# Experts' scores cut at each 32-query block, two tiles mirrored, values by pairs of tiles, in a fused attention and mixture-of-experts kernel

## The chip, the cores and the metric

The kernel runs on one core of one Trainium2 chip. The metric is the device time of one execution in microseconds. A core has a matrix engine (TensorE, PE in the profile), a vector engine (VectorE, DVE), a scalar engine (ScalarE, ACT), GpSimd (POOL) and SyncE (SP), which only issues transfers; their instruction streams run in order each and meet by semaphores. Matmuls write into PSUM, which has eight banks of 128 x 512 float32 numbers; VectorE and ScalarE read them from there.

## What is computed

Eight batches. First an attention with eight heads of 64 dimensions: 512 local queries look at neighbours within 32 positions and at 32 global keys, 32 global queries look at everything. Its output, 544 positions x 512 columns for each batch, goes into four "experts": causal attentions over all 544 positions, weighted by a gate that keeps the best two.

```python
# attention
s_ll = np.where(np.abs(pos[:, None] - pos[None, :]) <= 32, scale * q_l @ k_l.T, -1e9)
a_l = softmax(concat([scale * q_l @ k_g.T, s_ll]))
out_l = a_l @ concat([v_g, v_l])
out_g = softmax(scale * q_g @ concat([k_g, k_l]).T) @ concat([v_g, v_l])
# experts, on x = [out_g, out_l] with 512 columns
topk = two largest of x @ w_gate;  w = softmax over these two
for e in range(4):
    q, k, v = x @ wq[e], x @ wk[e], x @ wv[e]        # 64 columns each
    scores = where(causal, scale * q @ k.T, -1e9)
    ye = softmax(scores) @ v @ wo[e]
    out += (weight of e, 0 if not chosen) * ye
```

## The kernel before

The program is recorded as a list of operations, each with the engines that may run it, a cost, a priority and what it reads and writes (class `Plan`, lines 75 to 220). `place` then orders them: again and again it takes the operation that can start first by these costs, for TensorE also weighing the change of array shape and the distance to the oldest operation waiting. Buffers come from rings (`buf`, a tag and a number of copies); a ring with one copy makes the next writer wait until the last reader is done. The eight PSUM banks form one ring. So a change of costs, buffers or operations changes the whole order on every engine.

Work goes in 42 steps. One step handles one pair of heads of the local attention (32 pairs: load, transposes, scores L536, softmax L548 and L551, turning the probabilities L569, values L599, division L603) and, six steps later, a quarter of a batch of the experts. The experts of a batch are two pairs `c`; one matmul pair fills the two halves of the 128 rows with expert 2c and 2c+1. For a batch these are:

- `m_qk`, `m_v` (L733, L762, L773): projections, with weights split into a high and a low part.
- `m_scores` (L854): queries come in four tiles `i` of 128. A tile needs keys 0 to 128(i+1). Each tile's queries are four blocks `u` of 32; each block and each expert is one matmul, 32 queries standing (weights), the keys moving. The blocks lie in four groups of 32 columns of the array, the two experts in its two halves of rows, so eight matmuls sit on eight different parts of the array. Every block of a tile moves all 128(i+1) keys. Tiles 0 and 1 share a pair of banks (`TILES`, line 840).
- `m_softmax`: VectorE adds the mask and takes the minimum of the negated scores (L868), ScalarE takes the exponential (L872), VectorE the reciprocal (L875, L877), GpSimd scales by reciprocal and gate (L886; in the last pair GpSimd or VectorE).
- `m_ptrans`: turns the probabilities by 128-blocks (L569), into a ring `mptw` of three buffers, evicted by ScalarE (L277) or VectorE (L279).
- `m_av` (L921): for each tile and key block, one matmul of 64 value columns (weights) and 128 moving queries for each expert; then the result is split into a high and a low part (L288, L289).
- `m_tail_scores`, `m_tail_av` (L944, L984): the same for the 32 last positions of a batch, in one stacked tile. `m_gates`: the two best experts and their weights, on VectorE.
- `out_tile`, `m_out` (L1003): output projection, copied by ScalarE (L277) and written by one transfer of 128 rows that ScalarE issues (L1010).

Turned local probabilities (`ptw`) have two buffers. The raw weights go through `mptw` at the start.

## Time and profile before

| | |
|---|---|
| median of 3 runs (lowest, highest) | 503.62 us (503.43, 504.33) |
| profiled execution | 505.81 us |
| its span, first to last instruction | 504.0 us |
| TensorE busy, share of the span | 469.3 us, 93% |
| VectorE | 385.7 us, 77% |
| ScalarE | 324.4 us, 64% |
| GpSimd | 281.0 us, 56% |
| mean granted TensorE clock | 0.99 |
| L854, expert scores, TensorE busy | 43.7 us, 1024 instructions |
| L921, expert values, TensorE busy | 41.0 us, 640 instructions |

A float32 matmul stands in the profile as two instructions (two passes). Busy time of TensorE counts time in which at least one matmul is in flight; matmuls overlap, so what an operation costs is read from the distance of starts: the start of the next operation less its own start. In a timeline row the columns are start, length until the last end, engine, line, operation, what it writes and reads, the shape, and the number of instructions merged; in brackets the idle time before and what ended it. In a row of stages each engine has its busy time and its number of instructions.

### The profile page before, as it was taken

Reading aid. Unit: us, or ns where it says so; the run is one execution under the profiler, and the core shown is the slowest. Engines: PE = TensorE matmul, PEld = TensorE weight load, DVE = VectorE, ACT = ScalarE, POOL = GpSimd, SP = SyncE. Lnnn points to the kernel's source line nnn. Section 1 sums busy time; section 2 is a strip of 40 time slices with the busy share of each in tenths; the row PEclk is TensorE's granted clock in tenths of the full one; section 3 lists DMA queues with packets and bytes.
Section 4 is the critical chain, followed back from the end, with each engine's and each line's share of the span. In section 5 each row is a group of like instructions: output and inputs, shape, how many; then the busy total and the mean of one; then the engine's idle time right before and its main releaser. Section 6 shows DMA issues by size and latency. Waiting matters only on the chain.

```text
span 504.0 us, 25622 instructions
## 1 busy us (share of the span) xinstructions
PE 469.3 (93%) x10532; PEld 410.7 (81%) x10532; DVE 385.7 (77%) x1708; ACT 324.4 (64%) x1171; POOL 281.0 (56%) x520
## 2 busy tenths in 40 slices
PE   5787979799999999999989999999999999999985
PEld 3676968589889889889878889898988889888774
DVE  5889768989876997779956998769966976475570
ACT  1668636976756866768746867669757764563662
POOL 5879817869456492928656392837649261331220
PEclk9989989999999999999999999999999999999989
DMA  9955666654246324445146234453022100200203
GB/s 191 220 117 97 140 113 122 115 81 85 35 86 158 68 40 76 106 93 100 32 88 149 49 64 66 108 115 79 4 53 86 28 4 3 85 3 1 86 3 104
DMA packets 181620, 40.98 MB, mean 81 GB/s; under 512 B 176896, under 2 KB 176896, under 8 KB 181504
## 3 DMA queue, kind: packets, MB, share of 16 engines
q1 hardware_dynamic: 169488, 28.70, 31.0%
q10 hardware_dynamic: 12016, 10.65, 6.9%
q8 instruction: 82, 1.34, 1.1%
q14 instruction: 34, 0.28, 0.2%
HBM read 30.42 MB, written 8.91 MB: 78 GB/s over the span
## 4 chain that ended last, share of the span: by engine, by line
PE 76%; DVE 9%; DMA 4%; issue 4%; SPq 4%; ACT 3%; ACTq 1%; POOLq 0%; POOL 0%; DVEq 0%
PE bank L733 18%; PE bank L569 10%; PE bank L1003 9%; PE bank L762 8%; PE bank L921 7%; PE bank L599 6%; PE bank L854 5%; PE bank L536 4%; SPq L295 4%; DVE pm L868 3%; PE bank L703 2%; PE bank L663 2%; DMA qn<-in_q_l_dram 2%; DVE st L548 2%; PE bank L773 1%
## 5 line engine op out<-in xcount | busy, mean ns | idle before, releaser
L886 POOL TENSOR_SCALAR pm<-pm,msm,gate 128x512 f32<-128x512 f32 (+3 forms) x124 | 74.3, 612 | 101.1 <-DVE msm L877 56.1
L279 POOL COPY v<-v 32x512 f32<-32x512 f32 (+1 forms) x192 | 114.5, 596 | 19.8 <-DMA v<-in_v_l_dram 10.0
L551 ACT ACTIVATE st<-st,sm 128x128 f32<-128x128 f32 x256 | 99.7, 392 | 12.3 <-DVE sm L548 12.0
L279 POOL COPY v<-vg 32x640 f32<-32x640 f32 (+1 forms) x96 | 65.3, 680 | 37.6 <-PE bank L703 32.8
L872 ACT ACTIVATE pm<-pm,msm 128x512 f32<-128x512 f32 (+3 forms) x128 | 70.8, 554 | 18.9 <-DVE msm L868 17.8
L548 DVE CUSTOM_DVE_ANT_0 st<-bank,band 128x128 f32<-128x128 f32 x256 | 58.0, 284 | 3.2 <-PE bank L536 3.0
L868 DVE CUSTOM_DVE_ANT_0 pm<-bank,cmask 128x512 f32<-128x512 f32 (+3 forms) x128 | 55.2, 480 | 2.4 <-PE bank L854 2.1
L551 ACT ACTIVATION_READ_ACCUMULATOR st<-st,sm 128x1 f32 x256 | 48.6, 190 | 0.0
L854 PE MATMUL bank<-kt,qt 64*32 64x384 f32 (+3 forms) x1024 | 43.7, 433 | 1.0 <-issue 1.0
L921 PE MATMUL bank<-mptw,vt 128*64 128x128 f32 x640 | 41.0, 281 | 1.7 <-DVE xn L603 0.9
L599 PEld LDWEIGHTS bank<-v,ptw 128*32 128x32 f32 x2048 | 31.3, 112 | 12.8 <-issue 7.7
L536 PE MATMUL bank<-kd,qp 64*32 64x128 f32 x2048 | 39.4, 280 | 2.1 <-issue 2.1
L599 PE MATMUL bank<-v,ptw 128*32 128x64 f32 x2048 | 36.8, 223 | 4.4 <-DVE msm L868 2.5
L277 ACT COPY mptw<-bank 128x384 f32<-128x384 f32 (+1 forms) x50 | 24.2, 520 | 25.6 <-PE bank L921 18.4
L921 PEld LDWEIGHTS bank<-mptw,vt 128*64 128x64 f32 x640 | 36.6, 140 | 3.7 <-issue 2.3
L536 PEld LDWEIGHTS bank<-kd,qp 64*32 64x32 f32 x2048 | 32.1, 108 | 8.6 <-issue 5.0
L733 PE MATMUL bank<-xh,wk_hi 128*128 128x272 f32 x128 | 37.7, 294 | 0.0
L277 ACT COPY ptw<-bank 128x512 f32<-128x512 f32 x34 | 20.0, 594 | 27.1 <-PE bank L569 26.6
L733 PE MATMUL bank<-xl,wk_hi 128*128 128x272 f32 x128 | 37.0, 289 | 0.0
L733 PE MATMUL bank<-xl,wq_hi 128*128 128x272 f32 x128 | 36.9, 288 | 0.0
L733 PE MATMUL bank<-xh,wk_lo 128*128 128x272 f32 x128 | 36.9, 288 | 0.0
L733 PE MATMUL bank<-xh,wq_hi 128*128 128x272 f32 x128 | 36.8, 288 | 0.0
(159 smaller groups left out, 1321.1 us busy)
## 6 DMA issues: line engine op xcount, KB each, us to landing
out_dram<-ot ACTq DMA_DIRECT2D x32, 256.0 KB, 2.1
v<-in_v_l_dram SPq DMA_DIRECT2D x60, 120.0 KB, 2.9
kn<-in_k_l_dram SPq DMA_DIRECT2D x104, 64.0 KB, 2.8
qn<-in_q_l_dram SPq DMA_DIRECT2D x104, 64.0 KB, 2.8
v<-in_v_l_dram SPq DMA_DIRECT2D x31, 64.0 KB, 3.2
kn<-in_k_l_dram SPq DMA_DIRECT2D x8, 128.0 KB, 4.1
qn<-in_q_l_dram SPq DMA_DIRECT2D x8, 128.0 KB, 3.8
ot<-in_q_g_dram SPq DMA_DIRECT2D x8, 64.0 KB, 2.2
```

Of the source, the lines that this page charges most:

```text
L279: ENG[e].tensor_copy(out, in_)
L536: nc.tensor.matmul(sp[h].t[32 * g:32 * g + 32, 128 * t:128 * t + 128], qp.t[rows, 32 * u:32 * u + 32], kd.t[rows, c:c + 128], start=True, ...
L548: op("DVE", 211, lambda e, h=h, t=t, i=i: nc.vector.tensor_tensor_reduce(out=st.t[:, h, t], in0=sp[h].t[:, 128 * t:128 * t + 128], in1=ban ...
L551: op("ACT", 385, lambda e, h=h, t=t, i=i: nc.scalar.activation(st.t[:, h, t], st.t[:, h, t], AF.Exp, bias=sm.t[:, 0, i:i + 1], scale=-1.0, ...
L569: nc.tensor.transpose(two[y].t[:, k, :], block()[rows], ident[rows, rows])
L599: nc.tensor.matmul(xq.t[32 * g:32 * g + 32, t, h, :], pt.t[:, h, 32 * u:32 * u + 32], v.t[:, h, window(u), :], start=True, stop=True)
L733: nc.tensor.matmul(pp.t, w[:, ch, cols], x(part, ch)[:, n], start=(ch == 0 and w is hi and part == 0), stop=(ch == NCH - 1 and part == 1))
L854: nc.tensor.matmul(sp[x].t[32 * u:32 * u + 32, at:at + n], qt.t[rows, q0:q0 + 32], kt.t[rows, :n], start=True, stop=True)
L868: op("DVE", 78 + 1.04 * n, lambda e, x=x, at=at, n=n, i=i, s=s: nc.vector.tensor_tensor_reduce(out=pm.t[:, x, at:at + n], in0=sp[x].t[:, a ...
L872: op("ACT", 280 + 0.83 * n, lambda e, x=x, at=at, n=n, s=s: nc.scalar.activation(pm.t[:, x, at:at + n], pm.t[:, x, at:at + n], AF.Exp, bia ...
L886: lambda e, x=x, at=at, n=n, i=i, s=s: ENG[e].tensor_scalar(pm.t[:, x, at:at + n], pm.t[:, x, at:at + n], sm.t[:, 3, s:s + 1], gate.t[:, i ...
L921: nc.tensor.matmul(yp.t[64 * x:64 * x + 64, 128 * i - n0:128 * i - n0 + 128], vt.t[:, j, 64 * (2 * c + x):64 * (2 * c + x) + 64], flat[:, ...
```

## The change

1. Scores. A block `u` of tile `i` moves only 128i + 32(u+1) keys. In tiles 0 and 1 (`MIRRORED`) the blocks go to the column groups in reverse: block 3 in group 0, block 0 in group 3. Their rows stay reversed, block by block, through softmax, turning and values up to the output. A second mask (`rmask`) and a mirrored copy of two columns of the gates (four GpSimd copies a batch) go with that.
2. Tiles are grouped anew: tile 3 alone, tiles 2 and 0 in one pair of banks, tile 1 alone. Steps 0 and 2 of a batch take tile 3 and tile 1, steps 1 and 3 take tiles 2 and 0.
3. Values. Turned probabilities lie in two buffers with one copy each, `ptu` for tiles 3 and 2 and `ptl` for tiles 1 and 0, with the two tiles of a pair side by side for each key block. One matmul moves both tiles, 256 queries, where both need the key block, and 128 for the last one.
4. Output. Tiles 0 and 1 are written by four transfers of 32 rows each, issued by SyncE; tiles 2 and 3 as before by ScalarE.
5. At the start a zeroed buffer is multiplied into all eight banks, since parts of a bank are no longer written by every tile before they are read.
6. The raw weights go through the ring `pm`, the gate's weights through `msm`; `ptw` has one buffer; the costs given to the planner change with the work.

```diff
-    TILES = (((0, 0), (1, 128)), ((2, 0),), ((3, 0),))
+    TILES = (((3, 0),), ((2, 0), (0, 384)), ((1, 0),))
+    TURNS = ((3,), (2,), (1, 0))
+    MIRRORED = (0, 1)
...
-                n = 128 * (i + 1)
-                for u in range(4):
+                for g in range(4):
+                    u = 3 - g if i in MIRRORED else g
+                    n = 128 * i + 32 * (u + 1)
                     for x in range(2):
...
-                        nc.tensor.matmul(sp[x].t[32 * u:32 * u + 32, at:at + n], qt.t[rows, q0:q0 + 32],
+                        nc.tensor.matmul(sp[x].t[32 * g:32 * g + 32, at:at + n], qt.t[rows, q0:q0 + 32],
                                          kt.t[rows, :n], start=True, stop=True)
-        op("PE", 20 + 1.68 * sum(128 * (i + 1) for i, _ in TILES[t]), f, r=[kt, qt], w=sp, shape="scores")
+        op("PE", 20 + 1.68 * (464, 416, 208)[t], f, r=[kt, qt], w=sp, shape="scores")
...
-                for i in some:
-                    pt, where = pts[i]
-                    flat = pt.t.rearrange("p a j q -> p (a j) q")
-                    for j in range(i + 1):
+                for big, pt in zip(some, pts):
+                    at = Y_AT[big] - n0
+                    for j in range(big + 1):
+                        width = 256 if j < big else 128
                         for x in range(2):
-                            nc.tensor.matmul(yp.t[64 * x:64 * x + 64, 128 * i - n0:128 * i - n0 + 128],
+                            nc.tensor.matmul(yp.t[64 * x:64 * x + 64, at:at + width],
                                              vt.t[:, j, 64 * (2 * c + x):64 * (2 * c + x) + 64],
-                                             flat[:, where[x, i, j], :], start=(j == 0), stop=(j == i))
+                                             pt.t[:, x, 2 * j:2 * j + width // 128, :].rearrange("p s q -> p (s q)"),
+                                             start=(j == 0), stop=(j == big))
...
+        if i in MIRRORED:
+            dsts = [(out[b, 128 * i + 96 - 32 * g:128 * i + 128 - 32 * g, :], slice(32 * g, 32 * g + 32)) for g in range(4)]
+        else:
+            dsts = [(out[b, 128 * i:128 * i + 128, :], slice(0, 128))]
+        out_tile(y, lambda part, c: M[b, "yo"][part].t[:, c, at:at + 128], dsts, "SP" if i in MIRRORED else "ACT")
...
-            for x in {0: [(old, 1, 2)], 1: [(old, 1, 0), (old, 1, 1)], 2: [(cur, 0, 2)], 3: [(cur, 0, 0), (cur, 0, 1)]}[r]:
+            for x in {0: [(old, 1, 0), (old, 1, 2)], 1: [(old, 1, 1)], 2: [(cur, 0, 0), (cur, 0, 2)], 3: [(cur, 0, 1)]}[r]:
...
-        ptw = PR[k, "pt"] = buf("ptw", [128, 2, SL])
+        ptw = PR[k, "pt"] = buf("ptw", [128, 2, SL], 1)
...
+    def clear_banks():
+
+        zero = buf("pm", [128, 512], 3, F32R)
+        op("DVE", 350, lambda e: nc.vector.memset(zero.t.bitcast(F32), 0.0), w=[zero])
+        some = [ps([128, 512], "zero") for _ in range(8)]
+
+        def f(e):
+            for bank in some:
+                nc.tensor.matmul(bank.t, zero.t[:, :128], zero.t, start=True, stop=True)
+        op("PE", 2600, f, r=[zero], w=some)
```

Lines of the changed program differ: L854 becomes L870, L868 L885, L872 L889, L536 L544, L569 L577, L599 L607, L603 L611, L663 L671, L703 L711, L921 L955, L984 L1018, L1003 L1037, L1010 L1044.

The planner's order changes on all engines. Three places follow. TensorE first, in the middle of the program, where the values of a batch's second pair of experts are formed. Before, they follow a turn of probabilities (`ident,pm` turns an expert tile), with local values (L599), global values (L703) and the tail's values (L984) ahead, each in a bank of its own:

```order
L569 MATMUL bank_65<-ident,pm 128x64
L569 MATMUL bank_68<-ident,pm 128x64
L599 MATMUL bank_66<-v,ptw 32x64 x32
L703 MATMUL bank_71<-v,longt 32x64 x20
L984 MATMUL bank_67<-vt,longt 32x64 x20
L921 MATMUL bank_64<-mptw,vt 64x128 x20
L569 MATMUL bank_70<-ident,xn 128x64
L569 MATMUL bank_69<-ident,xn 128x64
```

The same place now:

```order
L544 MATMUL bank_65<-kd_79,qp 32x128
L544 MATMUL bank_64<-kd_79,qp 32x128
L607 MATMUL bank_71<-v,ptw 32x64 x32
L711 MATMUL bank_68<-v,longt 32x64 x20
L1018 MATMUL bank_71<-vt,longt 32x64 x20
L955 MATMUL bank_68<-ptl,vt 64x256 x2
L955 MATMUL bank_68<-ptl,vt 64x128 x2
L955 MATMUL bank_68<-ptu,vt 64x256 x6
L955 MATMUL bank_68<-ptu,vt 64x128 x2
```

The values now follow score matmuls (L544, the last of a bunch that began with tiles 3 and 1), and L1018 and L955 write into the banks that L607 and L711 used just before.

VectorE next: what follows the local masks (L548) in the bunch of score matmuls that also holds the tail's scores. Before, the masks of tiles 0 and 1 come first, in a bank of their own, then tile 2:

```order
L875 TENSOR_SCALAR msm<-msm 128x2
L519 STREAM_TRANSPOSE qp<-qn 128x512
L877 RECIPROCAL msm<-msm 128x2
L868 ISA pm,msm<-bank_66,cmask 128x128
L868 ISA msm 128x1
L868 ISA pm,msm<-bank_65,cmask 128x128
L868 ISA msm 128x1
L868 ISA pm,msm<-bank_66,cmask 128x256
L868 ISA msm 128x1
L868 ISA pm,msm<-bank_65,cmask 128x256
```

Now tiles 2 and 0 share a pair of banks, and both of a bank's masks must be through before it is free:

```order
L892 TENSOR_SCALAR msm<-msm 128x2
L527 STREAM_TRANSPOSE qp<-qn 128x512
L894 RECIPROCAL msm<-msm 128x2
L885 ISA pm,msm<-bank_64,cmask 128x384
L885 ISA msm 128x1
L885 ISA pm,msm<-bank_68,cmask 128x384
L885 ISA msm 128x1
L885 ISA pm,msm<-bank_64,rmask 128x128
L885 ISA msm 128x1
L885 ISA pm,msm<-bank_68,rmask 128x128
```

Tile 1's masks have moved ahead of the local ones, and bank_64 is released by its 128-wide mask, after both 384-wide ones.

Last, ScalarE at the end of the program (`ot` is an output tile; four transfers of 32 rows are the tail's). Before:

```order
L277 COPY ot<-bank_67 128x512
L277 COPY ot<-bank_69 128x512
L1010 DMA out_dram<-ot 32x512 x4
L1010 DMA out_dram<-ot 128x512
L277 COPY ot<-bank_68 128x512
L277 COPY ot<-bank_70 128x512
L1010 DMA out_dram<-ot 128x512 x2
L277 COPY ot<-bank_65 128x512
L1010 DMA out_dram<-ot 128x512
```

Now:

```order
L277 COPY ot<-bank_69 128x512
L1044 DMA out_dram<-ot 32x512 x4
L277 COPY ot<-bank_71 128x512
L277 COPY ot<-bank_68 128x512
L277 COPY ot<-bank_70 128x512
L1044 DMA out_dram<-ot 128x512
L277 COPY ot<-bank_67 128x512
L1044 DMA out_dram<-ot 128x512
```

Two tiles' transfers have left ScalarE; they stand as eight of 32 rows at the end of SyncE's list.

## What was predicted

> **What bounds the kernel now.** I read the page first, then the busy time by stage, then TensorE's and VectorE's timelines through one batch.
>
> ```profile
> span 504.0 us, 25622 instructions
> PE 469.3 (93%) x10532; PEld 410.7 (81%) x10532; DVE 385.7 (77%) x1708; ACT 324.4 (64%) x1171; POOL 281.0 (56%) x520
> PE 76%; DVE 9%; DMA 4%; issue 4%; SPq 4%; ACT 3%; ACTq 1%; POOLq 0%; POOL 0%; DVEq 0%
> ```
>
> TensorE is busy for 93% of the span and holds 76% of the chain. The shares differ by stage (columns: PE, weight loads, VectorE, ScalarE, GpSimd, then granted clock, DMA share and GB/s):
>
> ```profile
> 180.00:240.00 60.00, 58.78 (x1337) 52.55 (x1336) 49.91 (x220) 40.51 (x148) 37.23 (x68) 1.00 0.39 80
> 420.00:480.00 60.00, 60.00 (x964) 50.60 (x966) 35.20 (x133) 30.32 (x89) 15.55 (x29) 1.00 0.10 37
> 480.00:504.00 24.00, 16.76 (x213) 14.04 (x205) 8.80 (x35) 10.27 (x31) 2.65 (x4) 0.93 0.16 55
> ```
>
> In the middle TensorE is full, but VectorE is at 83%. From about 400 us, when local attention has run out, VectorE has room and TensorE alone sets the pace. The last 24 us are a chain of short steps. Inside a batch VectorE's load is bunched: every score bank must be drained by it. This is TensorE through the densest bunch of score matmuls, and the same bunch one batch later:
>
> ```profile
> 221.96 1.09 PE L854 MATMUL bank<-kt,qt 64*32 64x512 f32 x16
> 222.84 1.12 PE L536 MATMUL bank<-kd,qp 64*32 64x128 f32 x63
> 223.73 1.72 PE L854 MATMUL bank<-kt,qt 64*32 64x128 f32 x46
> 225.01 1.30 PE L944 MATMUL bank<-kt,qt 64*32 64x512 f32 x12
> 227.80 1.10 PE L599 MATMUL bank<-v,ptw 128*32 128x64 f32 x64 [0.50 <-DVE msm L868]
> 228.72 0.75 PE L703 MATMUL bank<-v,longt 128*32 128x64 f32 x40
> 229.40 2.40 PE L921 MATMUL bank<-mptw,vt 128*64 128x128 f32 x40
> 231.73 0.28 PE L569 MATMUL bank<-ident,st 64*128 64x64 f32 x2
> 279.41 1.09 PE L854 MATMUL bank<-kt,qt 64*32 64x512 f32 x16
> ```
>
> A batch takes 57.45 us (279.41 less 221.96). At 227.80 TensorE had waited for a bank that VectorE's masks (L868) had to free. VectorE in that bunch:
>
> ```profile
> 223.25 0.69 DVE L868 CUSTOM_DVE_ANT_0 pm<-bank,cmask 128x512 f32<-128x512 f32 x1
> 223.87 0.69 DVE L868 CUSTOM_DVE_ANT_0 pm<-bank,cmask 128x512 f32<-128x512 f32 x1
> 224.48 0.28 DVE L548 CUSTOM_DVE_ANT_0 st<-bank,band 128x128 f32<-128x128 f32 x1
> 226.24 0.70 DVE L519 STREAM_TRANSPOSE qp<-qn 128x512 f32<-128x512 f32 x1
> 226.91 0.27 DVE L868 CUSTOM_DVE_ANT_0 pm<-bank,cmask 128x128 f32<-128x128 f32 x1
> 228.01 0.56 DVE L868 CUSTOM_DVE_ANT_0 pm<-bank,cmask 128x384 f32<-128x384 f32 x1
> 228.96 0.17 DVE L554 TENSOR_SCALAR sm<-sm 128x8 f32<-128x8 f32 x1
> ```
>
> It runs without a gap. Start to start, a 512-wide mask costs 0.62 us (223.87 less 223.25), a 384-wide one 0.48 (228.01 to 228.96 for two), eight local masks and a small step 1.76 (224.48 to 226.24), the transpose with a small step 0.67. Two 128-wide and two 256-wide masks take 1.10 (226.91 to 228.01); at 0.21 and 0.35 that fits.
>
> **The change part by part.** TensorE's prices come from another stretch, where nothing waits:
>
> ```profile
> 258.40 2.40 PE L921 MATMUL bank<-mptw,vt 128*64 128x128 f32 x40
> 260.74 0.46 PE L569 MATMUL bank<-ident,xn 64*128 64x64 f32 x8
> 261.13 1.53 PE L854 MATMUL bank<-kt,qt 64*32 64x128 f32 x48
> 262.45 1.07 PE L663 MATMUL bank<-kd,kq 64*32 64x128 f32 x25
> 263.32 0.30 PE L536 MATMUL bank<-kd,qp 64*32 64x128 f32 x2
> 263.34 0.20 PE L663 MATMUL bank<-kd,kq 64*32 64x32 f32 x3
> ```
>
> Scores. The 512-wide tile takes 0.88 us (222.84 less 221.96), the three others, 768 columns, 1.32 (262.45 less 261.13): 2.20 us for 1280 columns, 1.72 ns a column. With each 32-query block cut at its own end and the mirrored tile behind the plain one, each of the four column groups moves 672 columns for tiles 3 and 1 and 416 for tiles 2 and 0: 1088, so 1.87 us and 0.33 less. That holds only if a group goes on while its neighbours still work. The last two rows speak for it: all of L663 stands ahead of L536 in the program, yet two matmuls of L536, on parts of the array that L663 leaves free, start at 263.32, before three of L663 at 263.34. So the price lies between 0 and -0.33 for each of 16 pairs of experts; I take the full -5.3 us. The Trainium skill says otherwise (TensorE: Matmul & The Clock Gate, Part 3, The mechanism): matmuls start and end in program order, with no reordering. By that rule the widest block holds the rest and this term is about 0; the two rows contradict it.
>
> Products with the values. 40 matmul passes become 24, but the columns moved stay 20 blocks of 128. They take 2.34 us (260.74 less 258.40); at the scores' 1.72 ns a column (0.86 a pass) 20 x 128 columns would be 2.20. So the gain is between 0 and -0.14 a pair, and a change of array shape lies in the same 0.14. I take -0.03, -0.5 in all.
>
> Changes of shape. The new order has 153 stretches of one array shape on TensorE where the old had 165. At 0 to 0.14 each, 0.1 taken: -1.2 us. TensorE's work falls by 7.0 us, about 0.9 a batch.
>
> Waits in the bunches. The old order had three bunches a batch, the new has two, each with tiles 3, 1, a local pair, tiles 2 and 0, and a second local pair (32 L536 matmuls, 0.89 us from 222.84 to 223.73). In the first, the values of the local pair need the bank of tiles 2 and 0, which is free after VectorE's 1.29 (223.25 less 221.96) + 1.23 (tile 3) + 0.70 (tile 1) + 1.76 + 0.67 + 0.96 (tile 2) + 0.21 = 6.8, with the signal 6.9 us. Before, that point came at 5.84 (227.80 less 221.96), without the second local pair. 6.9 less 0.9 is 6.0: no gain here, so 0.2 beside the 0.33 that I counted as saved, +0.5. In the second, the tail's product is put into the very bank that L611 must empty first (bank_71 in the order). L611 comes after 1.29 + 1.23 + 0.70 + 1.76 + 0.67 + 0.48 = 6.1 and takes about as long as a 512-wide mask: 6.8. TensorE, unhindered, is there after 1.87 + 1.78 (two local pairs) + 0.87 (L663, 262.45 to 263.32) + 0.92 (L599) + 0.68 (L703) = 6.1: a wait of 0.7 to 0.8. Then the output projection follows the expert product at once; its low half stands on VectorE behind the other half of the local masks, two 512-wide copies and the rest of tiles 2 and 0, by the same rates at 12.0, where TensorE is ready at 11.5: +0.5. Against this stand 0.5 of small waits that the old layout had. Sum +1.3 a batch, for the six batches beside which local attention runs: +7.8 us. It is the least certain term: +0.6 if ScalarE's copies let VectorE move up, +2.2 if the halves of a tile come later still.
>
> The end. These rows carry it:
>
> ```profile
> 482.50 0.60 ACT L872 ACTIVATE pm<-pm,msm 128x384 f32<-128x384 f32 x1
> 485.08 0.15 DVE L877 RECIPROCAL msm<-msm 128x2 f32<-128x2 f32 x1
> 484.46 0.52 PE L569 MATMUL bank<-ident,long 64*128 64x64 f32 x10 [1.10 <-ACT long L960]
> 486.15 0.61 PE L569 MATMUL bank<-ident,pm 64*128 64x64 f32 x12 [0.79 <-POOL pm L886]
> 487.79 3.60 PE L921 MATMUL bank<-mptw,vt 128*64 128x128 f32 x40
> 491.33 0.33 PE L630 MATMUL bank<-ident,turned 128*128 128x128 f32 x1
> 488.00:490.00 2.00, 2.00 (x22) 2.00 (x22) 0.54 (x2) 0.37 (x1) 0.00 (x0) 0.50 0.00 0
> 498.25 0.40 PE L1003 MATMUL bank<-wo_hi,yl 128*128 128x512 f32 x1
> 500.55 0.58 ACT L277 COPY ot<-bank 128x512 f32<-128x512 f32 x1 [0.63 <-ACT ot L277]
> 501.16 0.34 ACTq L1010 DMA_DIRECT2D out_dram<-ot  x1
> ```
>
> TensorE waits 1.10 and 0.79 us, and the clock is 0.50 while the last expert product runs, 3.54 us (487.79 to 491.33) for 2.34. That is 3.1 us that an earlier softmax could take away. The last exponential ends at 483.1, but its reciprocal starts at 485.08, behind two long VectorE steps. In the new order tile 3's scores of this pair stand ahead of the previous output projection, and the reciprocal directly behind the masks. I take -2.3, between 0 and -3.1. Behind the last matmul (498.65) ScalarE starts its last copy at 500.55, being busy with copies and five DMA issues; two of the five tiles now leave by SyncE, but as eight issues, 0.34 each by the last row, so I take only -0.4.
>
> The start:
>
> ```profile
> 3.45 0.66 PE L420 MATMUL bank<-ident,ot 64*128 64x64 f32 x4 [3.45 <-DMA ot<-in_k_g_dram]
> 10.18 1.08 PE L506 MATMUL bank<-ident,qn 128*128 128x128 f32 x4 [1.54 <-DMA qn<-in_q_l_dram]
> ```
>
> Clearing the banks is eight 512-wide matmuls, 3.2 us at the 0.40 of the row at 498.25 and 6.4 at half clock. TensorE has no data before 3.45 us and waits for loads again at 10.18, so at most the first transposes move. I take -0.3, between +1 and -1.5, since early matmuls may also raise the clock sooner.
>
> The rest costs nothing. The mirrored gates (four small GpSimd copies a batch, queued ahead of GpSimd's value copies and of the mirrored tiles' scaling) and the second mask's setup fall into the 23 us of 60 that GpSimd has free. Eight more SyncE issues a batch, 2.7 us, each waiting for a copy by ScalarE, stand ahead of loads that run two pairs ahead; without that lead a late load would hold VectorE's transposes by the issue time. The evictions of the turned probabilities keep their runs of 64 elements. Single buffers for them cost nothing where the product stands ahead of the next turn, as it does in the new order; elsewhere the eviction, and the next turn on its bank, would wait for the product.
>
> Sum: -5.3 - 0.5 - 1.2 + 7.8 - 2.7 - 0.3 = -2.2. The profiled execution took 505.81 us (span 504.0) and would take 503.6; the runs' median, 503.62, becomes 501.4.
>
> **The rivals.** (a) The bunches do not wait longer than before: without the +7.8 it is 493.6; half of it gives 497.5. For it: VectorE's total work is unchanged. Against: the gapless VectorE rows above, and eight banks for 14 uses before L607. Chance 0.21 for 497.5 or below. (b) Slower: VectorE's draining of the bunches becomes the bound. If each batch waits 1 us more than I count (2.3), that is +6: 507.4. It decides from 1.67 us a batch on, where the sum passes zero. For it: chain and wait row above run through L868. The Trainium skill warns of this (TensorEngine Tiling, PSUM Bottleneck): tiling speeds TensorE, not the emptying of PSUM; the wait at 227.80 agrees. Chance 0.23. (c) The groups keep to program order, so the cut scores save nothing: half of the 5.3 lies in waits anyway, so 504.0. The rows at 263.32 speak against it. Chance 0.05. This is what the in-order rule of the Trainium skill, weighed above, would give. (d) Gains and waits cancel within 1 us: 0.16. The forecast's own case, 498 to 502.6: 0.35.
>
> **How the numbers follow.** About 1 us (0.2%) is what a measurement here tells from no change. Faster by more: the forecast and (a), 0.56; same 0.16; slower (b) and (c), 0.28. The range, 496.5 to 506.5, leaves out the full form of (a) and the far end of (b), about 0.1 each.
>
> **What would show it.** Right: 1.87 us a pair for the scores, rows of a later tile starting on one column group before the earlier tile has ended on another; L611 releasing TensorE before the tail's product, the values' wait for L885, 57.8 us a batch; no half clock near the end. Wrong: a batch of 56.5 us or less (then the waits are mis-sized), or over 59, or scores still at 2.2.

## The result and the profile after

The kernel before took 503.2 us (median of six runs, 502.02 to 504.33), the changed kernel 508.4 (six runs, 505.35 to 509.63): a ratio of 1.0099, 95% interval 1.007 to 1.0127. The change made the kernel about 5 us slower. The forecast was 501.4, faster, with a range up to 506.5.

The profiled execution of the changed kernel, at 505.35 us, is the fastest of its six; that of before, at 505.81, lies above all six of its own. So the two profiles differ by 0.5 us while the medians differ by 5, and stages are compared below rather than spans. Two executions of one later kernel (the last experiments' blocks of 32) ran at a lower clock and over 1% longer than its others, one of them the profiled one; they are left out of its median, and its profile is not used. The page after: its span, TensorE's busy time, the chain that ended last by engine, and the queue that carries instructions (packets, MB, share of the 16 DMA engines).

```profile
span 502.9 us, 25258 instructions
PE 464.2 (92%) x10284; PEld 404.1 (80%) x10284; DVE 385.1 (77%) x1715; ACT 320.8 (64%) x1164; POOL 291.0 (58%) x558
PE 61%; DVE 13%; POOL 7%; issue 6%; DMA 5%; SPq 4%; ACT 3%; ACTq 1%; DVEq 0%; POOLq 0%
q8 instruction: 80, 1.31, 1.1%
```

TensorE's work fell by 5.1 us, from 469.3. But TensorE's share of the chain fell from 76 to 61%, VectorE's rose from 9 to 13, GpSimd's from 0 to 7 (only 2 in a second profile, below), and "issue", time in which an engine waits for nothing that the profile shows, from 4 to 6.

Three whole batches beside local attention, from the first matmul of the tail's value projection (L773, now L781) to the same matmul three batches later. First before, then after (columns: length, then busy time of TensorE, weight loads, VectorE, ScalarE, GpSimd, granted clock, DMA share, GB/s):

```profile
176.42:348.35 171.93, 167.66 (x3935) 149.46 (x3935) 141.11 (x624) 119.77 (x438) 103.67 (x190) 1.00 0.41 84
```

```profile
172.66:349.74 177.08, 165.59 (x3839) 146.94 (x3839) 138.95 (x628) 118.17 (x435) 106.17 (x201) 1.00 0.40 82
```

A batch took 57.3 us before and takes 59.0 now, though TensorE is busy for 0.7 us less in it. The other batches differ less or the other way: the first two took 61.7 and 57.7 us before and take 59.0 and 58.3 now, in these two profiles. What TensorE waited for in these windows (total us, times, longest), before:

```profile
PE bank L599 <- DVE msm L868: 1.8, 3, 0.7
PE bank L984 <- issue: 1.4, 1, 1.4
PE bank L921 <- issue: 0.5, 1, 0.5
PE bank L599 <- issue: 0.2, 1, 0.2
```

and after:

```profile
PE bank L711 <- issue: 4.4, 3, 1.6
PE bank L638 <- DVE ptw L279: 2.3, 3, 0.8
PE bank L607 <- DVE msm L885: 2.2, 3, 0.8
PE bank L544 <- issue: 1.2, 3, 0.5
PE bank L607 <- issue: 0.9, 1, 0.9
```

Waits for VectorE rose from 1.8 to 4.5 us in three batches, waits for "issue" from 2.1 to 6.5. This is TensorE through the second bunch of one of these batches, each row a run of like matmuls with their number:

```profile
247.75 1.37 PE L870 MATMUL bank<-kt,qt 64*32 64x416 f32 x32
248.90 1.11 PE L544 MATMUL bank<-kd,qp 64*32 64x128 f32 x63
249.78 0.40 PE L870 MATMUL bank<-kt,qt 64*32 64x288 f32 x1
249.79 0.27 PE L544 MATMUL bank<-kd,qp 64*32 64x128 f32 x1
249.79 0.91 PE L870 MATMUL bank<-kt,qt 64*32 64x288 f32 x26
250.48 0.27 PE L671 MATMUL bank<-kd,kq 64*32 64x128 f32 x1
...
252.11 1.07 PE L544 MATMUL bank<-kd,qp 64*32 64x128 f32 x54 [0.27 <-issue]
253.11 1.10 PE L607 MATMUL bank<-v,ptw 128*32 128x64 f32 x64
254.03 0.33 PE L711 MATMUL bank<-v,longt 128*32 128x64 f32 x9
255.76 0.60 PE L711 MATMUL bank<-v,longt 96*32 96x64 f32 x28 [1.40 <-issue]
256.20 0.77 PE L1018 MATMUL bank<-vt,longt 128*32 128x64 f32 x39
256.90 0.87 PE L955 MATMUL bank<-ptl,vt 128*64 128x256 f32 x8
...
261.47 0.44 PE L638 MATMUL bank<-ident,turned 128*128 128x128 f32 x2 [0.78 <-DVE ptw L279]
```

At 255.76 TensorE had stood still for 1.40 us in the middle of L711, with nine of that operation's matmuls done and no operand missing. From the wait that ended at 252.11 to that one there are 54 + 64 + 9 = 127 matmuls, each with a weight load: about 256 instructions. The page's instruction queue carries 80 packets of 16 KB. With all entries of TensorE's queue in the trace numbered in order of start (matmuls, weight loads and the few control instructions), nearly all its "issue" waits of at least 0.3 us end at one place in 256. This is a count over the trace's records, for the two kernels and for the runs of the next section; the fetches are the packets of the instruction queue:

```
kernel                    waits   us   at 193 or 194 mod 256   closest two fetches, us
before                      10    9.5           9                      3.36
changed kernel              13   12.6          13                      3.29
changed, second profile     15   15.3          15                      3.31
half of VectorE's masks     19   20.3          19                      3.32
64 matmuls ahead            16   16.1          15                      3.31
local scores two blocks      5    3.8           5                      3.34
same, kernel before          5    3.1           4                      3.38
scores uncut                13   14.2          13                      3.27
two blocks and uncut         7    6.3           6                      3.32
old handing out             15   15.3          14                      3.29
blocks of 64 (last)          9    8.3           9                      3.37
blocks of 64, before        11    9.9          10                      3.36
clearing alone, before      11   10.7          11                      3.31
```

The fetches fit these waits one by one: all 143 that end at this place end 1.15 to 1.86 us after the transfer of a packet has ended (median 1.39). In the changed kernel's first profile the 13 packets concerned start 0.6 to 2.8 us after the block before theirs was entered, and that block then takes 3.2 to 5.4 us, wait included; no block passes in under 3.1. The few waits elsewhere stand 2 us or more after any transfer: one of 0.8 us in the kernel before, which leaves 8.7 of its 9.5.

So the theory tested below, called the code theory: TensorE's program comes in blocks of 256 instructions. The next block is mostly fetched only once the present one has been entered, and 3 to 4 us pass until it can be run. Where 128 matmul passes and their weight loads take less than that, TensorE waits at the block's end. A local pair's scores are 64 matmuls in 0.88 us, its values another 64 in 0.92, so the bunches are where this binds, and the new order makes two dense bunches a batch of three looser ones. The rival, the VectorE theory, is the forecast's rival (b): VectorE's draining of the score banks sets the length of the bunches. The Trainium skill describes blocks of this size (Runtime: NRT & Kernel Launch, Instruction fetch mechanics), fetched by the sequencer's own queue, and calls their cost mostly hidden; the size agrees with the packets, the hiding doesn't agree with these waits.

### The profile page after: what moved, and what is told of

The parts are those of the page before. It is cut to its first block, busy times and chain, and to the rows that moved or that the text cites. A ratio compares the mean times of both kernels' runs of the same rounds, so it can differ in the third digit from the quotient of the medians.

```text
span 502.9 us, 25258 instructions
## 1 busy us (share of the span) xinstructions
PE 464.2 (92%) x10284; PEld 404.1 (80%) x10284; DVE 385.1 (77%) x1715; ACT 320.8 (64%) x1164; POOL 291.0 (58%) x558
## 4 chain that ended last, share of the span: by engine, by line
PE 61%; DVE 13%; POOL 7%; issue 6%; DMA 5%; SPq 4%; ACT 3%; ACTq 1%; DVEq 0%; POOLq 0%
PE bank L741 17%; PE bank L1037 9%; PE bank L577 8%; PE bank L770 7%; POOL v L279 6%; PE bank L607 5%; PE bank L955 4%; SPq L295 4%; DVE pm L885 4%; PE bank L870 4%; PE bank L544 2%; DVE st L556 2%; DMA qn<-in_q_l_dram 2%; DMA v<-in_v_l_dram 2%; PE bank L711 1%
## 5 line engine op out<-in xcount | busy, mean ns | idle before, releaser
L905 POOL TENSOR_SCALAR pm<-pm,msm,gate 128x512 f32<-128x512 f32 (+3 forms) x125 | 75.6, 620 | 79.7 <-DVE msm L894 61.0
L889 ACT ACTIVATE pm<-pm,msm 128x512 f32<-128x512 f32 (+3 forms) x128 | 70.5, 552 | 20.8 <-DVE msm L885 20.6
L279 POOL COPY v<-vg 32x640 f32<-32x640 f32 (+1 forms) x96 | 67.6, 704 | 22.5 <-PE bank L711 17.6
L544 PE MATMUL bank<-kd,qp 64*32 64x128 f32 x2048 | 42.1, 275 | 4.9 <-issue 4.4
L607 PE MATMUL bank<-v,ptw 128*32 128x64 f32 x2048 | 39.0, 229 | 6.3 <-DVE msm L885 3.0
L506 POOL COPY kd<-kq 128x160 f32<-128x160 f32 x32 | 10.1, 320 | 57.2 <-PE bank L671 35.2
L607 PEld LDWEIGHTS bank<-v,ptw 128*32 128x32 f32 x2048 | 33.0, 115 | 12.3 <-DVE msm L885 4.1
L544 PEld LDWEIGHTS bank<-kd,qp 64*32 64x32 f32 x2048 | 32.7, 106 | 9.8 <-issue 6.9
L885 DVE CUSTOM_DVE_ANT_0 pm<-bank,cmask 128x512 f32<-128x512 f32 (+1 forms) x64 | 37.5, 615 | 2.2 <-PE bank L870 1.6
L870 PE MATMUL bank<-kt,qt 64*32 64x96 f32 (+15 forms) x1024 | 37.8, 393 | 1.1 <-issue 0.7
L770 PE MATMUL bank<-wv_hi,xh 128*128 128x260 f32 x128 | 36.4, 285 | 0.5 <-ACT ptw L277 0.5
L741 PE MATMUL bank<-xh,wq_lo 128*128 128x272 f32 x128 | 36.9, 288 | 0.0
```

Of the source, the lines that this page charges most:

```text
L279: ENG[e].tensor_copy(out, in_)
L544: nc.tensor.matmul(sp[h].t[32 * g:32 * g + 32, 128 * t:128 * t + 128], qp.t[rows, 32 * u:32 * u + 32], kd.t[rows, c:c + 128], start=True, ...
L607: nc.tensor.matmul(xq.t[32 * g:32 * g + 32, t, h, :], pt.t[:, h, 32 * u:32 * u + 32], v.t[:, h, window(u), :], start=True, stop=True)
L741: nc.tensor.matmul(pp.t, w[:, ch, cols], x(part, ch)[:, n], start=(ch == 0 and w is hi and part == 0), stop=(ch == NCH - 1 and part == 1))
L770: nc.tensor.matmul(pv.t, x(part, ch)[:, 128 * i:128 * i + 128], w[:, ch, :], start=(ch == 0 and part == 0 and w is hi), stop=(ch == NCH - ...
L870: nc.tensor.matmul(sp[x].t[32 * g:32 * g + 32, at:at + n], qt.t[rows, q0:q0 + 32], kt.t[rows, :n], start=True, stop=True)
```

## The experiments

**The changed kernel again.** No edit.

> The changed kernel itself once more, for a second profiled execution: the first had a span of 502.9 us, but the timed runs' spans went from 502.9 to 507.2. Code theory (TensorE's program reaches it in blocks of 256 instructions, of which only the next is fetched ahead, and no two fetches of the first trace start less than 3.29 us apart; every wait of TensorE of over 0.5 us for nothing that the profile shows stands at such a block's end): a longer execution differs by these waits, and they stand at the same instructions; 13.7 us of them in the first, 15 to 18 in one that takes 507. VectorE theory (its drain of the score banks holds TensorE): the waits for VectorE differ, 9 us in the first, 12 to 14 in one of 507, those at the blocks' ends don't. Time 506 to 509 for both.

506.63 us (505.14 to 508.28; ratio 1.0076, interval 1.005 to 1.0103). The second profiled execution had a span of 506.4, 3.5 longer than the first. TensorE's longest waits in it:

```profile
PE bank L711 <- issue: 6.3, 5, 1.7
PE bank L544 <- issue: 5.0, 8, 1.1
PE bank L607 <- DVE msm L885: 2.7, 4, 0.8
PE bank L607 <- issue: 2.7, 3, 1.1
PE bank L638 <- DVE ptw L279: 2.6, 4, 0.8
```

In the first execution the same rows were 4.6, 4.4, 3.0, 2.2 and 2.6. The three for "issue" grew by 2.8 in all, the two for VectorE fell by 0.3, and the waits of 0.3 us and more stand again at the blocks' ends. All "issue" waits together grew from 13.8 to 16.3 us, most of the 3.5 us that set these two executions apart.

**Fewer instructions, same columns**, in the changed kernel and in the one before. Half of the local scores are computed with wrong queries.

```diff
-            for t in range(4):
+            for t in (0, 2):
...
-  nc.tensor.matmul(sp[h].t[32 * g:32 * g + 32, 128 * t:128 * t + 128],
-                   qp.t[rows, 32 * u:32 * u + 32], kd.t[rows, c:c + 128],
+  nc.tensor.matmul(sp[h].t[32 * g:32 * g + 32, 128 * t:128 * t + 256],
+                   qp.t[rows, 32 * u:32 * u + 32], kd.t[rows, c:c + 256],
```

> Local attention's score matmuls two blocks at a time: half as many, each 256 columns wide instead of 128, so the columns moved stay and 2048 of TensorE's 20600 instructions go (8 blocks of 81). Half of the local scores are thereby computed with the wrong queries. Order and costs of the plan are as in the changed kernel. Code theory: the waits at the blocks' ends in the bunches shrink by half a block a local pair where they bind, so 8 to 12 us less than the changed kernel, 497 to 501. VectorE theory: VectorE's work is untouched, so within 1 us of the changed kernel.

> The same edit to the kernel before (half of the local scores wrong). Code theory: it has 15.7 us of waits at blocks' ends where the changed kernel has 19.8, in three lighter bunches a batch, so it gains less: 4 to 7 us, 496 to 499, and the distance between the two kernels falls from 5.2 to at most 2 us. VectorE theory: unchanged, 503, and the distance stays 5.

The changed kernel: 493.44 us (492.42 to 493.91; ratio 0.9807, interval 0.9782 to 0.9832). The kernel before: 495.34 (493.21 to 496.64; 0.9844, 0.9816 to 0.9872). The edit took 13.2 us from the changed kernel (beside its 506.63 of the same session) and 7.9 from the other, more than expected of both. (The 15.7 and 19.8 us in the second expectation are more than the 9.5 and 12.6 of the table; counted at the weight loads, the idle time at the block ends is 15.2 and 19.2.) These matmuls themselves cost the same: in the lightened changed kernel a pair's 32 run from 244.62 to 245.49.

```profile
244.62 1.14 PE L544 MATMUL bank<-kd,qp 64*32 64x256 f32 x32
245.49 0.94 PE L870 MATMUL bank<-kt,qt 64*32 64x288 f32 x29
```

That is 0.87 us for 32 where 64 took 0.88 (248.90 to 249.78). What went are the waits; the lightened changed kernel's longest:

```profile
PE bank L607 <- DVE msm L885: 3.2, 4, 0.8
PE bank L1018 <- issue: 2.7, 5, 1.0
...
PE bank L1018 <- DVE xn L611: 1.7, 4, 0.5
```

The wait for VectorE's masks (L607 for L885) is as long as before, and the kernel is 13 us faster. With the code lightened the changed kernel is the faster of the two by 1.9 us; the two intervals overlap, so the sign is likely and not settled. That the forecast's gain, 2.2, lies near it is chance: it set 10.0 us of savings against 7.8 of waits for VectorE.

**Scores uncut.** Every block has its tile's full width again; order and costs stay.

```diff
-                    n = 128 * i + 32 * (u + 1)
+                    n = 128 * (i + 1)
```

> The changed kernel with every block's scores at the full width of its tile again (128, 256, 384 or 512 columns), mirrored tiles, pairs, order and costs kept. The trace's prices put 0.33 us a pair of experts on it, 5.3 us in all. Code theory: the bunches end when their code has come, so in the six batches beside local attention the wider matmuls fill waits, and only the start and the last two batches pay: 1 to 3 us more than the changed kernel. Rival (the cut saved its full price, and something else cost more): 4.5 to 5.5 us more, 513.

508.03 us (505.39 to 510.16; ratio 1.0096, 1.0063 to 1.0129), 1.4 above the changed kernel of the same session, with overlapping intervals. The cut's 5.3 us of passes are worth 1.4 or less in time. The same edit on the lightened kernel:

> The changed kernel with both edits of the first four runs: local scores two blocks at a time (half of them wrong) and the experts' scores at full width. With the code lightened the bunch is no longer held by it everywhere, so the cut should be worth more than the 0.5 us that it was worth in the changed kernel. Code theory: 2 to 5 us above the 493.4 of the kernel with the cut, 495.5 to 498.5. If the cut is hidden by something else (VectorE's drain of the same banks): within 1 us of 493.4.

495.25 us (495.01 to 497.81; ratio 0.9862, 0.9834 to 0.9889), 1.8 above 493.44: just under the expected 2 to 5. The cut is worth little more there, so the code isn't all that swallows it. The waits for VectorE at L607 are 3.2 us with and without the cut; what else hides the remainder was not tried.

**The experts' scores handed out as before.** Only the steps at which the tiles are asked for go back.

```diff
-  {0: [(old, 1, 0), (old, 1, 2)], 1: [(old, 1, 1)], 2: [(cur, 0, 0), (cur, 0, 2)], 3: [(cur, 0, 1)]}
+  {0: [(old, 1, 0)], 1: [(old, 1, 2), (old, 1, 1)], 2: [(cur, 0, 0)], 3: [(cur, 0, 2), (cur, 0, 1)]}
```

> The changed kernel with its experts' scores handed out over the steps as the kernel before had them: tile 3 alone in one step, tiles 2, 0 and 1 in the next (it was tiles 3 and 1, then 2 and 0). Everything else of the change stays; the plan makes a new order of it. Code theory: the blocks of 256 instructions that pass in under 3.6 us become fewer, some 3 to 8 us of the waits at their ends go: 500 to 504. If the cost lies in the cut, the mirrored tiles or the pairs of tiles themselves, it stays: 506 to 509.

503.31 us (501.14 to 506.43; ratio 1.0007, 0.9984 to 1.003): the loss is gone. It came with the new handing out, not with the cut, the mirrored tiles, the pairs or the clearing, which all stay here. The trace bears out the expected mechanism in the middle of the program alone. The same three batches:

```profile
176.02:348.42 172.40, 167.35 (x3837) 144.93 (x3838) 136.66 (x621) 122.12 (x441) 106.63 (x202) 1.00 0.42 84
```

A batch takes 57.5 us, with 2.5 us of "issue" waits in the three where the changed kernel has 6.5, and 1.4 of waits for VectorE for 4.5. Over the whole program the waits at block ends didn't fall: 14.1 us, beside 12.6 and 15.3 in the changed kernel's two profiles, because the start and the first two batches hold more of them. What fell there are the waits for VectorE, to 5.0 us from 12.9 and 11.9. So this run shows where the loss came from, but not that the block ends alone made it.

**VectorE's masks halved.** ScalarE's exponential reads a constant over the full width, so its own work stays; the experts' probabilities are wrong.

```diff
-  out=pm.t[:, x, at:at + n], in0=sp[x].t[:, at:at + n], in1=mask,
+  out=pm.t[:, x, at:at + n // 2], in0=sp[x].t[:, at:at + n // 2], in1=mask[:, :n // 2],
...
-  pm.t[:, x, at:at + n], pm.t[:, x, at:at + n], AF.Exp, ...
+  pm.t[:, x, at:at + n].rearrange("p (j k) -> p j k", k=128),
+  ident.unsqueeze(1).to_broadcast([128, n // 128, 128]), AF.Exp, ...
```

> The changed kernel with VectorE's work on the experts' scores halved: it masks half of each tile's columns, and ScalarE takes the exponential of a constant over the whole width, so its work stays; the probabilities are wrong. About 16 us of VectorE's 385 go, all of them in the bunches. VectorE theory: TensorE's waits for VectorE there (3.0 us for the reciprocals behind the masks, 2.6 us at the transposes of the tail, 0.6 for the scaled heads) go, and the time falls by 5 to 9 us, to 499 to 502. Code theory: the bunch still needs its blocks, so a wait that goes at one place comes back at the next block's end: 0 to 3 us less, 504 to 507.

507.98 us (505.77 to 511.49; ratio 1.0108, 1.0073 to 1.0143): no gain at all. Its page and its waits:

```profile
PE 461.9 (92%) x10284; PEld 402.3 (80%) x10284; DVE 368.5 (73%) x1715; ACT 321.3 (64%) x1164; POOL 292.0 (58%) x558
```

```profile
PE bank L711 <- issue: 7.1, 5, 1.7
PE bank L544 <- issue: 5.2, 8, 1.4
PE bank L607 <- issue: 4.9, 5, 1.6
PE bank L638 <- DVE ptw L279: 2.4, 4, 0.7
```

VectorE lost 16.6 us of work and TensorE its 3.0 us of waits for the masks. The three waits for "issue" grew from 11.2 to 17.2. In the bunch shown above the same matmul, nine into L711, now waits 1.67 us instead of 1.40:

```profile
255.85 0.60 PE L711 MATMUL bank<-v,longt 96*32 96x64 f32 x28 [1.67 <-issue]
```

TensorE reaches the block's end sooner and the block comes no sooner. This removes the drain of the score banks as the cause of the loss. (The wait of L638, for the eviction of turned probabilities, is no mask's and stayed: 2.4 us beside 2.6.)

**Blocks moved by half a block.** 64 small matmuls ahead of the bank clearing.

```diff
+            for _ in range(64):
+                nc.tensor.matmul(some[0].t[:, :32], zero.t[:, :128], zero.t[:, :32], start=True, stop=True)
```

> The changed kernel with 64 more matmuls of 32 columns ahead of the bank clearing, 128 instructions, which is half a block; they can delay the start by up to 3 us, the rest of the order is the same. Code theory: all block ends move by half a block: the waits that stood 194 instructions into the count stand at other matmuls (those of 1.5 to 1.9 us at L711 vanish there and appear at L544 or L607, half a block off), still at 194 modulo 256 of all instructions; the time changes by -3 to +6 us beyond the start. VectorE theory, or any cause in the data: the waits stay at the same matmuls and the time moves by the start's delay alone, 0 to 3 us.

512.71 us (510.02 to 515.03; ratio 1.0198, 1.0167 to 1.0228). The time tells little, since the added matmuls took far longer than expected (below). The places tell much; the bunch shown above, in this kernel:

```profile
263.50 1.04 PE L544 MATMUL bank<-kd,qp 64*32 64x128 f32 x54
264.47 0.35 PE L607 MATMUL bank<-v,ptw 128*32 128x64 f32 x9
265.28 0.93 PE L607 MATMUL bank<-v,ptw 128*32 128x64 f32 x52 [0.46 <-issue]
266.00 0.22 PE L711 MATMUL bank<-v,longt 128*32 128x64 f32 x1
266.03 0.23 PE L607 MATMUL bank<-v,ptw 128*32 128x64 f32 x3
266.06 0.77 PE L711 MATMUL bank<-v,longt 128*32 128x64 f32 x39
267.07 0.69 PE L1018 MATMUL bank<-vt,longt 128*32 128x64 f32 x33 [0.24 <-DVE xn L611]
269.28 0.32 PE L1018 MATMUL bank<-vt,longt 128*32 128x64 f32 x7 [1.52 <-issue]
```

The waits at L544 and L711 are gone from here. They stand in L607 and L1018, 63 and 64 matmuls later, with 52 + 1 + 3 + 39 + 33 = 128 matmuls between them. Counted in instructions they stand where they stood, at 193 or 194 modulo 256. Nothing in the data moved, only the count.

**Towards a better version.** The old handing out while local attention runs, the new one from the step where it has run out; then the same with the experts' scores in blocks of 64 queries, half as many matmuls for 32 more columns.

```diff
+  ({0: [(old, 1, 0), (old, 1, 2)], 1: [(old, 1, 1)], 2: [(cur, 0, 0), (cur, 0, 2)], 3: [(cur, 0, 1)]} if not at(s) else
+   {0: [(old, 1, 0)], 1: [(old, 1, 2), (old, 1, 1)], 2: [(cur, 0, 0)], 3: [(cur, 0, 2), (cur, 0, 1)]})
```

```diff
-                for g in range(4):
-                    u = 3 - g if i in MIRRORED else g
-                    n = 128 * i + 32 * (u + 1)
+                for g in range(2):
+                    u = 1 - g if i in MIRRORED else g
+                    n = 128 * i + 64 * (u + 1)
```

> The kernel with the old handing out of the experts' scores (503.3 us) while local attention runs, and the change's (tiles 3 and 1, then 2 and 0) from the step on where it has run out. The end of the changed kernel had no wait of over 0.4 us and no half clock, that of the other one a wait of 2.23 us and a last expert product of 3.57 us for 2.31. Code theory: the dense bunches are gone in the batches and the last ones hold no local matmuls, so both gains stand: 2.5 to 3.5 us less than 503.3, 499.8 to 500.8. If the changed order brings its waits into the last two batches too: 502.5 to 505.

> The same, with the experts' scores in blocks of 64 queries instead of 32: half as many of these matmuls, 1024 instructions or 4 blocks less, and 32 columns more a column group for each of the two halves of the tiles, 0.11 us a pair of experts by the trace's 1.72 ns, 1.8 us in all. The mirrored tiles are turned and written by 64 rows. Code theory: 8 blocks less were worth 14.1 us in the changed kernel and 7.9 in the kernel before, so 4 blocks in the same bunches are worth 3 to 6 us, less the columns: 1 to 4.5 us less than the kernel in blocks of 32, 496 to 499.5. If instructions cost nothing: 1 to 2 us more, 501.5 to 502.5.

In blocks of 32: 501.2 us (median of ten runs; ratio 0.9972, 0.9941 to 1.0004), 2.1 below 503.31 where 2.5 to 3.5 were expected, and not told apart from the kernel before. In blocks of 64: 498.91 (497.05 to 499.72; ratio 0.9925, 0.9895 to 0.9954), 2.3 less, within the expected 1 to 4.5, though it moves more columns. It is faster than both kernels: 0.75% below the one before. The same blocks of 64 in the kernel before, at full width, hence with the same columns:

```diff
-                for u in range(4):
+                for u in range(2):
...
-                        q0 = 128 * i + 32 * u
-                        nc.tensor.matmul(sp[x].t[32 * u:32 * u + 32, at:at + n], qt.t[rows, q0:q0 + 32],
+                        q0 = 128 * i + 64 * u
+                        nc.tensor.matmul(sp[x].t[64 * u:64 * u + 64, at:at + n], qt.t[rows, q0:q0 + 64],
```

> The kernel before with its experts' scores in blocks of 64 queries at the same full width: the same columns, 512 matmuls and 1024 instructions less (4 blocks), nothing else changed. Code theory: about half of what 8 blocks gave it, 3 to 5 us, 498.5 to 500.5. VectorE theory, or if instructions are free: 503 within 1 us; more if a change between arrays cut by 32 and by 64 columns costs as much as other changes of shape (0.1 us for each of some 60 changes, 509).

500.49 us (ratio 0.9961, 0.9936 to 0.9987): 2.2 us less than its kernel before of 502.7, below the expected 3 to 5, on the code theory's side of zero. Its profile, of its slowest execution, doesn't show the mechanism over the whole program: 9.9 us of waits in the table beside the kernel before's 9.5, while the waits for VectorE are 2.0 us beside 8.2. In the three middle batches the "issue" waits are 1.0 us for 2.1. Where this gain comes from stays open.

**The bank clearing alone**, put into the kernel before:

```diff
+    clear_banks()
     p1_batch(0)
```

> The kernel before with the bank clearing alone (memset, eight matmuls, nothing else). On record is -0.3 us, between +1 and -1.5; the changed kernel's first batch came 1.7 us sooner by the trace. If that comes from the clearing (TensorE's clock rises sooner): 501.5 to 502. If from the order: 503 to 504.

502.29 us (ratio 1.0004, 0.9981 to 1.0027): no difference that can be measured.

## Why the prediction was wrong

**The step that failed** is "Waits in the bunches". It asked only when VectorE would empty the banks, and priced the denser bunches at 1.3 us a batch of such waits. The waits for VectorE did grow, by 0.9 us a batch ((4.5 - 1.8) / 3), but they don't decide: halving VectorE's masks left the time where it was. The waits that the sum had no term for are those at the ends of instruction blocks, 1.5 us a batch more ((6.5 - 2.1) / 3). The profile of before offered one: 4% of the chain was "issue", in a row that the prediction quoted and passed over, and nine of ten such waits stood at the same place in 256 there too. The same three batches in the profiles of the experiments (us; waits in the three together):

```
kernel                       a batch   "issue"   VectorE
before                         57.3      2.1       1.8
changed                        59.0      6.5       4.5
changed, second profile        59.2      6.8       4.5
scores uncut                   59.2      6.3       4.5
half of VectorE's masks        59.1      9.9       2.1
64 matmuls ahead               58.4      5.3       2.7
old handing out                57.5      2.5       1.4
local scores two blocks        56.9      1.4       3.7
clearing alone, before         58.0      4.0       2.0
```

The length of a batch follows the waits for "issue" and not those for VectorE: with the masks halved the latter are about as short as before and the batch as long as in the changed kernel; with half as many local score matmuls they are long and the batch is short. That the code makes the batches of the new order longer is shown by these runs. How the 3.4 to 5.2 us of the whole program divide is not: outside these batches all waits for "issue" run from 7.0 us (clearing alone) to 13.8 (old handing out), and from 7.3 to 9.5 between the two profiles of the changed kernel.

**Scores, -5.3: the price was right, the gain wasn't there.** In the bunch above tiles 3 and 1 take 1.15 us (247.75 to 248.90) and tiles 2 and 0 about 0.70 (249.78 to 250.48): 1.85 us a pair, forecast 1.87. The groups do run at their own pace: tile 2's first matmul (249.78) starts before the last of L544 (249.79), which stands ahead of it. By the in-order rule of the Trainium skill (TensorE: Matmul & The Clock Gate, Part 3, The mechanism) the price would have stayed 2.2 us; the trace contradicts it again. But undoing the cut costs 1.4 us, not 5.3. That a bunch which ends with its code, or behind another wait, gives nothing back for shorter matmuls fits this; the kernel with half as many local score matmuls gave back only 1.8, so the code is not the whole of it.

**Values, -0.5, and changes of shape, -1.2.** The product now runs from 256.90 to 259.22 (with the "turn" behind it), 2.3 us as forecast (2.34 before). The changes of shape were not measured by themselves.

**The batch.** Forecast 57.8 us, with "over 59" as a sign of being wrong; it is 59.0 in the first profile's three batches. Of the signs named, the values' wait for L885 came (2.2 us in three batches). The wait of the tail's product for L611 came only in small, 0.24 us in the shifted kernel, and more once the code was lightened: 1.7 us in four waits, up to 0.5, where 0.7 to 0.8 each was forecast. In the changed kernel the code's wait in L711, directly ahead of it, seems to cover it. A wait that the prediction did not name came as well: L638's for VectorE's eviction of `ptw`, 2.3 us in the three batches.

**The end, -2.7.** Its mechanism came in the main as forecast:

```profile
485.44 0.52 PE L577 MATMUL bank<-ident,long 64*128 64x64 f32 x10
485.80 1.43 PE L577 MATMUL bank<-ident,pm 64*128 64x64 f32 x24
487.16 0.77 PE L1018 MATMUL bank<-vt,longt 128*32 128x64 f32 x40
487.86 1.73 PE L955 MATMUL bank<-ptu,vt 128*64 128x256 f32 x16
489.42 0.82 PE L955 MATMUL bank<-ptl,vt 128*64 128x256 f32 x8
```

The waits of 1.10 and 0.79 us ahead of these turns are gone, and the last product takes 2.31 us (487.86 to 490.17) at the full clock, where it took 3.54 at half. Only the waits can be put down to the change for certain. The kernel before with the clearing alone has both waits (1.09 and 0.79) and yet ran this product at the full clock, in 2.33 us; of the five profiles that keep a long wait here, four have the half clock, of the eight used that don't, none. The size was smaller than forecast: with the grouped order in the last batches alone the kernel came about 2 us below the one with the old handing out throughout, and even that isn't told apart from zero by the intervals.

**The start, -0.3, and the rest, nil.** The clearing alone changed nothing measurable. The kernel with the old handing out holds all of the rest (mirror copies, second mask, eight SyncE issues, single buffers) and the gains, and equals the kernel before, so the rest may cost something up to the size of those gains; it was not separated. TensorE's busy time in its three batches is 167.35 us beside 167.66 before and 165.59 in the changed kernel, so most of the shorter passes don't show there; why stays open.

**The rivals.** Rival (b) gave 507.4, close to the measured time, but by luck: the halved masks rule its mechanism out, since VectorE's draining doesn't set the bunches' length here. Rival (a), waits that don't grow, gave 493.6 to 497.5; it took the wide local scores, 493.4, to get there. Rival (c), groups in program order, fails by the 1.85 us above.

## What to carry to other kernels

When TensorE's program is long and unrolled, count instructions as well as columns: here 128 matmul passes (64 float32 matmuls) with their weight loads didn't get through in under 3.1 us, and those that would have been done sooner waited for their successors. "Issue" waits that recur at one place in 256 instructions are the sign. Half as many local score matmuls at the same columns took most of these waits away (from 12.6 to 3.8 us); spreading the bunches took them away in the middle of the program only; shorter matmuls or less work on VectorE didn't. Packing like work together to save changes of shape had this price here.

## What the hardware showed

TensorE's instruction blocks of 16 KB, which nothing in the kernel names, held it for 8.7 us of the kernel before and 12.6 and 15.3 us of two executions of the changed one (waits of 0.3 us and more). A block's transfer took only 0.9 to 1.9 us, but the waits ended 1.15 us or more after it, and no two fetches in these traces started less than 3.27 us apart (the kernel with its scores uncut).

The 64 added matmuls of 32 columns, all into one place of one bank, took 13.84 us, 216 ns each, where 32 columns were expected to take almost nothing:

```profile
1.45 13.84 PE L1192 MATMUL bank<-pm 128*128 128x32 f32 x64 [1.45 <-DVE pm L1187]
```

Why one took so long was not tried.
